# Chunk attention and an expert layer on one core: the first tile's row sums, transposes and casts in another order

## The chip, the cores and the metric

The kernel runs on one core of one Trainium2 chip. The metric is the device time of one execution in microseconds (us). Times inside a profile are us from the start of the profiled span.

## What is computed

The reference works on `q`, `k` and `v` of shape (8, 8, 576, 64): batch, heads, tokens, head size. Attention is taken inside chunks of 64 tokens; its result, with the heads side by side, is the input of an expert layer with an exact GELU.

```python
scores = (q_c @ k_c.T) / sqrt(64)          # per chunk of 64 tokens
attn   = exp(scores - max) / sum(exp(...)) # the kernel leaves the max out
x      = (attn @ v_c)                      # -> 4608 tokens x 512
out    = gelu(x @ w_in) @ w_out            # 512 -> 2048 -> 512
```

Inputs and output are f32; the kernel multiplies in bf16.

## The kernel before

**Tiles.** The 4608 tokens are worked in nine tiles of 512: eight tiles hold eight chunks of one batch entry each, the ninth holds the last chunk of all eight. A tile goes through attention and then the expert layer: sixteen output blocks of `x @ w_in` with GELU on ScalarE (`mm1_slot`), then the second product. While TensorE does the expert layer of one tile, the other engines load, cast, transpose and scale the next one. The first tile has nothing before it to hide behind: its attention runs alone, while the weights arrive and are cast.

**Order.** The program is written out by hand inside `tc.manual_schedule()`: each engine executes its instructions in the order in which they are emitted, and all loads go out on SyncE's queue. A tile pool with a fixed number of buffers makes an instruction wait for the last reader of the buffer it takes. In PSUM there are three pools: `ps_mm` (3 banks; expert outputs, k transposes of the first tile, warm matmuls), `ps_tp` (2 banks) and `ps_at` (3 banks).

**The first tile's attention.** The eight heads form four groups `g` of two heads. For each group:

- `cast_qk` turns the f32 arrivals of q and k into bf16 (VectorE or GpSimd, `DV` and `PO`).
- `att_T` (made by `att_units` as `T[0]` ... `T[7]`; even ones are q, odd ones k) transposes on TensorE (`transposed`, L166, four matmuls of 128x128) and copies the result from PSUM to `qT` (VectorE) or `kT` (ScalarE), L174.
- `att_S` (L376) computes 16 score blocks of 64x64 on 64x64 parts of the array, and ScalarE takes the exponentials into `pT` (two instructions, L380). Two groups share a pair of PSUM banks.
- The row sums. For groups 0 and 1 `att_sum` multiplies with a block matrix of ones (L387), so that every row of the output holds the sums; VectorE transposes in blocks of 32x32 (L392), takes the reciprocal of one column (L396) and transposes it back, spread over 32 columns, into `rcs` (L397). For groups 2 and 3 `att_sum_pe` makes the sums lie along partitions (L415, four matmuls with two moving columns), VectorE takes the reciprocal (L420), TensorE spreads it by f32 matmuls with an identity (L427) and ScalarE copies it to `rcs` (L430).
- `att_av` (L441) multiplies with V, two groups in a pair of banks, and `att_x` (L449) scales by `rcs` into `x`. For groups 0 and 1 this goes in two halves, `ns` being the pairs of chunks: (0, 1), then (2, 3).

`keep_warm(n)` (L725) issues `n` matmuls of zeros, 128x512, whose output nobody reads. `cast_v_plain` (L152) casts V, one block of 128 keys after the other.

**After it.** `win[c](i, engine)` casts block `i` of the c-th quarter of `w_in` (L706). `mm1_begin(0, 3)` (L493) starts the expert layer with three output blocks, whose inner index `ks` is the group of `x`: first `ks` 0 and 1 for all three, then 2 and 3. `mm1_slot` (L481) does the other thirteen.

Of the kernel before, what the change touches and what calls it, by code (L numbers as in the profile page):

```python
# [11 lines left out]
def kernel(  # L12
# [9 lines left out]
    nc = tc.nc  # L22
    P = 128
    f32 = mybir.dt.float32
    bf16 = mybir.dt.bfloat16
    Act = mybir.ActivationFunctionType

    B, H, S, D = q.shape
    CH = 64
# [3 lines left out]
    G = H // 2  # L33
# [3 lines left out]
    CT = NC - 1  # L37
    MT = CT * CH
    NT = B + 1
    KS = d_model // P  # L40
# [4 lines left out]
    consts = ctx.enter_context(tc.tile_pool(name="consts", bufs=1))  # L45
    rest = consts.tile([P, 512], bf16, name="rest")
    nc.vector.memset(rest[:], 0.0)
    ident = consts.tile([P, P], bf16, name="ident")
    make_identity(nc, ident)
    ones_bd = consts.tile([P, P], bf16, name="ones_bd")  # L50
    nc.vector.memset(ones_bd[:], 0.0)
    nc.vector.memset(ones_bd[0:CH, 0:CH], 1.0)
    nc.vector.memset(ones_bd[CH:P, CH:P], 1.0)

    ones_r = consts.tile([P, 2], bf16, name="ones_r")
    nc.gpsimd.memset(ones_r[:], 0.0)
    nc.gpsimd.memset(ones_r[0:CH, 0:1], 1.0)
    nc.gpsimd.memset(ones_r[CH:P, 1:2], 1.0)
    ident_f = consts.tile([P, P], f32, name="ident_f")
    nc.gpsimd.tensor_copy(ident_f[:], ident[:])  # L60
    QD = P // G
    ones_c = consts.tile([P, QD], bf16, name="ones_c")
    nc.gpsimd.memset(ones_c[:], 0.0)
# [14 lines left out]
    work = ctx.enter_context(tc.tile_pool(name="work", bufs=3))  # L78
    xpool = ctx.enter_context(tc.tile_pool(name="xpool", bufs=2))
    hpool = ctx.enter_context(tc.tile_pool(name="hpool", bufs=1))  # L80
    hsum = ctx.enter_context(tc.tile_pool(name="hsum", bufs=1))
    ypool = ctx.enter_context(tc.tile_pool(name="ypool", bufs=3))
    ps_mm = ctx.enter_context(tc.tile_pool(name="ps_mm", bufs=3, space=bass.MemoryType.PSUM))
    ps_tp = ctx.enter_context(tc.tile_pool(name="ps_tp", bufs=2, space=bass.MemoryType.PSUM))
    ps_at = ctx.enter_context(tc.tile_pool(name="ps_at", bufs=3, space=bass.MemoryType.PSUM))
# [8 lines left out]
    tiles = [dict() for _ in range(NT)]  # L94
# [49 lines left out]
        for n in range(CT // 2):  # L144
            nc.sync.dma_start(tiles[t]["vf"][:, :, n], v[t, :, P * n:P * (n + 1), :].rearrange("h key d -> key h d"))

    def cast_v_plain(t, copy, ns=range(CT // 2)):
        st = tiles[t]
        if 0 in ns:
            st["v"] = ld.tile([P, H, CT // 2, D], bf16, tag="v", name="v_nat")  # L150
        for n in ns:
            copy(st["v"][:, :, n], st["vf"][:, :, n])  # L152

    def place(r, i):

# [2 lines left out]
    def cast_qk(t, nm, g, copy):  # L158
        st = tiles[t]
        copy(st[nm][:, g].rearrange("p j r d -> p r j d"), st[nm + "f"][:, 2 * g:2 * g + 2])  # L160
# [16 lines left out]
    def parity_blocks(ns=range(4)):  # L177

        for n in ns:
            for a in range(2):  # L180
                for r in range(2):
                    c = a ^ r
                    yield n, r, c, 2 * n + c, slice(CH * r, CH * (r + 1)), slice(CH * c, CH * (c + 1))
# [186 lines left out]
    def att_S(t, g):  # L370

        st = tiles[t]
        if g % 2 == 0:
            st["s_ps"] = [ps_at.tile([P, 2, CT // 2, CH], f32, tag="at", name="s_ps") for _ in range(2)]
        for n, r, c, i, rs, cs in parity_blocks():
            nc.tensor.matmul(st["s_ps"][r][cs, g % 2, n], st["kT", g][rs, i, :], st["qT", g][rs, i, :],  # L376
                             start=True, stop=True, tile_position=(CH * r, CH * c))
        st["pT", g] = work.tile([P, 2, CT // 2, CH], bf16, tag="pT", name="pT", bufs=8)
        for r in range(2):
            nc.scalar.activation(st["pT", g][:, r], st["s_ps"][r][:, g % 2], Act.Exp, scale=scale)  # L380

    def att_sum(t, g, later=False):
        pT = tiles[t]["pT", g]
        sum_ps = ps_at.tile([P, MT], f32, tag="at", name="sum_ps")
        for c in range(2):
            for r in range(2):
                nc.tensor.matmul(sum_ps[CH * r:CH * (r + 1)].rearrange("p (n c e) -> p n c e", c=2, e=CH)[:, :, c],  # L387
                                 ones_bd[:, CH * c:CH * (c + 1)], pT[:, r], start=True, stop=True,
                                 tile_position=(0, CH * r))
        t1 = work.tile([P, NB, 32], f32, tag=f"y_{1 + t}", name="t1", bufs=1)  # L390
        rc = rc_of(t, g).rearrange("p (n e) -> p n e", e=32)
        nc.vector.transpose(t1[:], sum_ps[:].rearrange("p (n e) -> p n e", e=32))  # L392

        def rest_of_it():
            r1 = work.tile([P, NB], f32, tag="r1", name="r1", bufs=2)
            nc.vector.reciprocal(r1[:], t1[:, :, 0])  # L396
            nc.vector.transpose(rc, r1[:].to_broadcast([P, NB, 32]))  # L397
        if later:
            return rest_of_it
        rest_of_it()  # L400

    def att_rc(t, g):

# [1 line left out]
        rc = work.tile([P, NB, 32], f32, tag="rc", name="rc", bufs=4)  # L405
        nc.vector.transpose(rc[:], rb[:, g].to_broadcast([P, NB, 32]))  # L406
        tiles[t]["rc", g] = rc

    def att_sum_pe(t, g):

        pT = tiles[t]["pT", g]
        sT = ps_at.tile([P, 2, MT // P // 2, 2], f32, tag="at", name="sT")
        for r in range(2):
            for m in range(2):
                nc.tensor.matmul(sT[:, r, m], pT[:, r, 2 * m:2 * m + 2].rearrange("p n e -> p (n e)"), ones_r[:],  # L415
                                 start=True, stop=True)
        rr = work.tile([P, 2, MT // P // 2, 2], f32, tag="rr", name="rr", bufs=2)

        def inverse():
            nc.vector.reciprocal(rr[:], sT[:])  # L420

        def spread():
            rc_ps = ps_mm.tile([P, CT // 2, 2, CH], f32, tag="mm", name="rc_ps")
            for m in range(2):
                for c in range(2):
                    for r in range(2):
                        nc.tensor.matmul(rc_ps[CH * r:CH * (r + 1), 2 * m:2 * m + 2, c],  # L427
                                         rr[:, r, m, c:c + 1].to_broadcast([P, D]), ident_f[:],
                                         start=True, stop=True, tile_position=(0, CH * r))
            nc.scalar.copy(rc_of(t, g), rc_ps[:].rearrange("p n c e -> p (n c e)"))  # L430
        return inverse, spread

    def att_av(t, g2, ns):

# [9 lines left out]
    def att_x(t, g2, c, ns):  # L444

        st = tiles[t]
        def part(p):
            return p.rearrange("p g (n c e) -> p g n c e", c=2, e=CH)[:, :, ns[0]:ns[-1] + 1, c]
        nc.vector.tensor_tensor(part(st["x"][:, 2 * g2:2 * g2 + 2]), st["av", g2][c][:, :, ns[0]:ns[-1] + 1],  # L449
                                part(st["rcs", g2][:]), op=mybir.AluOpType.mult)  # L450

    def rc_of(t, g):

        if g % 2 == 0:
            tiles[t]["rcs", g // 2] = hsum.tile([P, 2, MT], f32, tag=f"s{3 + g // 2}", name="rcs")
        return tiles[t]["rcs", g // 2][:, g % 2]

    NB = MT // 32
    DV, AC, PO = nc.vector.tensor_copy, nc.scalar.copy, nc.gpsimd.tensor_copy
# [26 lines left out]
    def mm1_begin(t, n):  # L486

        st = tiles[t]
        st["h"] = hpool.tile([P, FF, MT], bf16, tag="h", name="h")
        h_ps = [ps_mm.tile([P, MT], f32, tag="mm", name="h_ps") for _ in range(n)]  # L490
        order = [(f, ks) for k2 in range(2) for f in range(n) for ks in (2 * k2, 2 * k2 + 1)]
        for f, ks in order:
            nc.tensor.matmul(h_ps[f][:], w_in_sb[:, ks, f * P:(f + 1) * P], st["x"][:, ks, :],  # L493
                             start=(ks == 0), stop=(ks == KS - 1))
        for f in range(n):
            nc.scalar.activation(st["h"][:, f, :], h_ps[f][:], Act.Gelu)
# [225 lines left out]
    def keep_warm(n):  # L722
        warm = ps_mm.tile([P, MT], f32, tag="mm", name="warm")
        for _ in range(n):
            nc.tensor.matmul(warm[:], rest[:, 0:P], rest[:], start=True, stop=True)  # L725
# [3 lines left out]
    def act_table(func):  # L729
        nc.scalar.activation(act_scratch[:], rest[:, 0:1], func)  # L730

    with tc.manual_schedule():
# [4 lines left out]
        win = [load_w_in(c, 2 if c < 2 else 1) for c in range(NWC - 1)]  # L737
        act_table(Act.Exp)
        keep_warm(7)
        T = att_units(0, DV, AC)  # L740
        for nm, g in (("k", 0), ("k", 1), ("q", 2), ("k", 2), ("q", 3), ("k", 3)):
            cast_qk(0, nm, g, PO)
        cast_v_plain(0, PO)
        cast_qk(0, "q", 0, DV)
        T[0]()
        cast_qk(0, "q", 1, DV)
# [1 line left out]
        keep_warm(3)  # L748
        T[2]()
        T[3]()  # L750
        att_S(0, 0)
        keep_warm(1)
        T[4]()
        r0 = att_sum(0, 0, True)
        att_S(0, 1)
        keep_warm(1)
        T[5]()
        r0()
        keep_warm(1)
        att_S(0, 2)  # L760
        T[6]()
        r1 = att_sum(0, 1, True)
        T[7]()
        i2, p2 = att_sum_pe(0, 2)
        i2()
        att_S(0, 3)
        r1()
        p2()
        i3, p3 = att_sum_pe(0, 3)
        i3()  # L770
        att_av(0, 0, (0, 1))
        for c in range(2):
            att_x(0, 0, c, (0, 1))
        p3()
        att_av(0, 0, (2, 3))
        for c in range(2):
            att_x(0, 0, c, (2, 3))
# [5 lines left out]
        win[0](0, PO)  # L783
        win[0](1, AC)
        act_table(Act.Gelu)
        win[0](2, PO)
        win[0](3, DV)
        mm1_begin(0, 3)
        load_qk(1, "q")
        wout.append(load_w_out(1))  # L790
# [22 lines left out]
        T = att_units(1, AC, AC)  # L813
# [47 lines left out]
        for t in range(1, NT):  # L861
            e1, e2 = {}, {}
            n = t + 1
# [71 lines left out]
```

## Time and profile before

| | |
|---|---|
| Runs, device us | 279.21, 279.69, 281.28; median 279.69 |
| Profiled execution | 281.07 us, of which the span in the profile is 279.3 us |
| Mean granted TensorE clock | 0.993 of full |
| Busy, share of the span | TensorE 96%, VectorE 60%, ScalarE 55%, GpSimd 31% |
| Second half of the chain before the expert layer | first expert matmul at 19.16 us |

Busy times are from the profiled execution, which can differ a little from the median run. The profile calls TensorE's matmuls PE and its weight loads PEld, VectorE DVE, ScalarE ACT, GpSimd POOL and SyncE SP. A line number such as L376 is a line of the kernel before. An entry like `DVE qT L174` is the instruction of VectorE that writes the tile `qT` at line 174; `xN` is how many of them were merged; the text in brackets names what ended the idle time before it. The chain in order of time gives start, duration and instruction of the work that ended last, followed back from the end.

### The profile page before, as it was taken

How to read it: one execution, taken by the hardware profiler on the slowest of the kernel's cores; microseconds unless marked ns; L12 is line 12 of the kernel's file. 1: busy time of each engine (PE TensorE's matmuls, PEld its weight loads, DVE VectorE, ACT ScalarE, POOL GpSimd, SP SyncE). 2: the span in 40 equal slices, each digit the busy share in tenths (PEclk: the TensorE clock that was granted, in tenths of full speed). 3: DMA queues.
4: the chain of work that ended last, by engine and by line, in shares of the span. 5: the costliest groups of instructions: out<-in, count | busy, mean ns of one | idle time of the engine just before them, and what ended most of it. 6: DMA issues, size and time to landing. Idle time of an engine off the chain costs nothing.

```text
span 279.3 us, 6704 instructions
## 1 busy us (share of the span) xinstructions
PE 269.3 (96%) x2721; PEld 159.6 (57%) x2721; DVE 166.6 (60%) x357; ACT 154.7 (55%) x290; POOL 87.7 (31%) x180
## 2 busy tenths in 40 slices
PE   7779999999999999999999999999999999999993
PEld 2454454444444444448844884588458745874682
DVE  2574226701956395995777577758775877434532
ACT  2467755778646765763566256725672565116500
POOL 2735675521630802740580372026402120000000
PEclk9799999999999999999999999999999999999999
DMA  6999999998899987999898829895841310040005
GB/s 202 248 365 404 395 387 247 260 257 237 244 230 266 236 192 212 299 210 241 232 239 211 228 92 232 202 186 156 210 99 40 116 38 2 0 153 0 0 2 151
DMA packets 118063, 53.92 MB, mean 193 GB/s; under 512 B 93456, under 2 KB 112912, under 8 KB 118032
## 3 DMA queue, kind: packets, MB, share of 16 engines
q1 hardware_dynamic: 117712, 52.97, 71.2%
q10 hardware_dynamic: 320, 0.52, 0.5%
q8 instruction: 21, 0.34, 0.5%
q14 instruction: 10, 0.08, 0.1%
HBM read 36.70 MB, written 9.44 MB: 165 GB/s over the span
## 4 chain that ended last, share of the span: by engine, by line
PE 92%; DVE 3%; DMA 2%; SPq 0%; issue 0%; ACT 0%; POOL 0%
PE h_ps L481 43%; PE y_ps L536 27%; PE y_ps L630 10%; PE y_ps L654 4%; DMA arrival<-in_k_dram 2%; PE av_ps L299 2%; PE s_ps L229 2%; PE tp L166 1%; PE h_ps L493 1%; DVE x L367 1%; PE rc_ps L427 1%; DVE rc L406 1%; SPq L112 0%; PE s_ps L376 0%; PE warm L725 0%
## 5 line engine op out<-in xcount | busy, mean ns | idle before, releaser
L481 PE MATMUL h_ps<-x,w_in_sb 128*128 128x512 bf16 x564 | 123.4, 379 | 0.4 <-DVE x L367 0.4
L484 ACT ACTIVATE h<-h_ps 128x512 bf16<-128x512 f32 x141 | 83.8, 597 | 55.7 <-PE h_ps L481 55.6
L481 PEld LDWEIGHTS <-w_in_sb 128*128 128x128 bf16 x564 | 55.1, 98 | 66.2 <-issue 0.7
L536 PEld LDWEIGHTS <-h_s 128*128 128x128 bf16 x384 | 36.8, 98 | 4.5
L160 POOL CAST q_nat<-arrival 128x512 bf16<-128x512 f32 x33 | 20.8, 668 | 57.0 <-DMA arrival<-in_q_dram 37.5
L536 PE MATMUL y_ps<-w_t,h_s 128*128 128x256 bf16 x288 | 33.7, 273 | 0.0
L630 PE MATMUL y_ps<-w_out_sb,h 128*128 128x512 bf16 x144 | 32.5, 380 | 0.0
L536 PEld LDWEIGHTS <-h 128*128 128x128 bf16 x288 | 28.2, 98 | 4.5
L251 DVE STREAM_TRANSPOSE pt<-pT 128x256 f32<-128x256 f32 x28 | 12.2, 437 | 27.8 <-ACT pT L236 27.8
L160 POOL CAST k_nat<-arrival 128x512 bf16<-128x512 f32 x34 | 20.1, 626 | 16.2 <-DMA arrival<-in_k_dram 11.8
L207 POOL CAST v_nat<-arrival 128x1024 bf16<-128x1024 f32 x14 | 14.4, 1040 | 31.5 <-DMA arrival<-in_v_dram 31.5
L516 DVE TENSOR_TENSOR h_s<-h 128x512 bf16<-128x512 bf16 (+1 forms) x30 | 11.2, 372 | 21.3 <-ACT h L484 21.3
L536 PE MATMUL y_ps<-w_out_sb,h 128*128 128x256 bf16 x192 | 22.9, 273 | 0.0
L630 PEld LDWEIGHTS <-h 128*128 128x128 bf16 x144 | 13.4, 98 | 15.6 <-issue 0.2
L730 ACT ACT_TABLE_LOAD x16 | 20.5, 1283 | 1.0 <-PEq L919 0.7
L254 DVE TENSOR_REDUCE part<-pt 128x16 f32<-128x512 bf16 x28 | 19.2, 686 | 1.0
L306 DVE TENSOR_TENSOR x<-av_ps,rc 128x512 bf16<-128x512 f32 x28 | 17.9, 684 | 3.1 <-PE av_ps L299 2.5
L569 ACT COPY y_sb<-y_ps 128x512 f32<-128x512 f32 x5 | 2.9, 586 | 26.1 <-PE y_ps L536 26.1
L236 ACT ACTIVATE pT<-s_ps 128x512 bf16<-128x512 f32 x28 | 14.4, 606 | 1.5 <-PE s_ps L229 1.5
L261 POOL COPY part<-part 32x32 f32<-32x32 f32 x40 | 9.2, 230 | 13.8 <-DVE part L254 12.1
L654 PE MATMUL y_ps<-w_out_sb,h 128*128 128x512 bf16 x48 | 11.8, 379 | 0.3 <-ACT h L484 0.3
L517 DVE TENSOR_TENSOR h_s<-h_s,h 128x512 bf16<-128x512 bf16 (+1 forms) x30 | 11.2, 372 | 1.0
(102 smaller groups left out, 248.8 us busy)
## 6 DMA issues: line engine op xcount, KB each, us to landing
out_dram<-y_sb SPq DMA_DIRECT2D x32, 256.0 KB, 2.6
arrival<-in_q_dram SPq DMA_DIRECT2D x7, 1024.0 KB, 6.7
arrival<-in_k_dram SPq DMA_DIRECT2D x24, 256.0 KB, 6.3
arrival<-in_v_dram SPq DMA_DIRECT2D x42, 128.0 KB, 3.1
arrival<-in_moe_w_out_dram SPq DMA_DIRECT2D x4, 1024.0 KB, 12.4
arrival<-in_v_dram SPq DMA_DIRECT2D x8, 256.0 KB, 6.3
arrival<-in_moe_w_in_dram SPq DMA_DIRECT2D x4, 512.0 KB, 6.2
arrival<-in_moe_w_in_dram SPq DMA_DIRECT2D x2, 1024.0 KB, 10.2
```

Of the source, the lines that this page charges most:

```text
L160: copy(st[nm][:, g].rearrange("p j r d -> p r j d"), st[nm + "f"][:, 2 * g:2 * g + 2])
L207: copy(st["v"][:, r::2], st["vf"][:, r::2])
L236: nc.scalar.activation(pT[:].rearrange("p u (c j) -> p u c j", j=J), s_ps[g2][c][:].rearrange("p u (j c) -> p u c j", j=J), Act.Exp, scale ...
L251: nc.vector.transpose(pt[:].rearrange("p n e u -> p (n e u)").bitcast(f32).rearrange("p (n e) -> p n e", e=32), st["pT", 2 * g2 + c][:].re ...
L254: nc.vector.tensor_reduce(st["part", g2][:, c, :, :, 0], pt[:].rearrange("p n e u -> p n u e"), axis=mybir.AxisListType.X, op=mybir.AluOpT ...
L306: nc.vector.tensor_tensor(x.rearrange("p n (e u) -> p n e u", u=2), st["av"][g2][c][:].rearrange("p n (e u) -> p n e u", u=2), st["rc", 2 ...
L481: nc.tensor.matmul(h_ps[a][:], w_in_sb[:, ks, o * P:(o + 1) * P], st["x"][:, ks, :], start=(ks == 0), stop=(ks == KS - 1))
L484: nc.scalar.activation(st["h"][:, f_of(t, f + a), :], h_ps[a][:], Act.Gelu)
L536: nc.tensor.matmul(out[m], lhs[:, f, m * P:(m + 1) * P], rhs[:, f, :], start=fresh and f == 0 and (m == 0 or len(out) == 3), stop=(f == FH ...
L630: nc.tensor.matmul(y_ps[:], st["h"][:, f, ms * P:(ms + 1) * P], w_out_sb[:, f, :], start=(f == 0), stop=(f == FF - 1))
L654: nc.tensor.matmul(tiles[t]["y_ps", ms][:], tiles[t]["h"][:, f, ms * P:(ms + 1) * P], w_out_sb[:, f, :], start=(f == 0), stop=False)
L730: nc.scalar.activation(act_scratch[:], rest[:, 0:1], func)
```

## The change

Only the first tile's part is changed.

- The row sums of all four groups are computed by `att_sums`: 32 matmuls for each group whose weights are 32 tokens of `pT` (128x32) and whose moving operand is `ones_r` (two columns). They write 32-partition blocks in the layout in which VectorE can take the reciprocal and spread it with one 32x32-block transpose (`att_spread`). `att_sum`, `att_sum_pe` and the constants `ones_bd` and `ident_f` go.
- The third group's k is cast by VectorE instead of GpSimd; the transposes `T[4]` to `T[6]` stand nearer to the casts, and the warm matmuls are placed anew (`keep_warm(1)` at four places of the attention instead of three).
- The last block of V is cast half by GpSimd and half by ScalarE.
- The third block of the first `w_in` quarter is cast by VectorE and the fourth by GpSimd (before: GpSimd and VectorE).
- In `mm1_begin` the third output block does its four matmuls at the end.

```diff
+    def att_sums(t, g):
+        st = tiles[t]
+        pT = st["pT", g]
+        st["sums", g] = ps_mm.tile([P, CT // 2, 2, 2], f32, tag="mm", name="sums_ps")
+        for n in range(CT // 2):
+            for e in range(2):
+                for s in range(G):
+                    nc.tensor.matmul(st["sums", g][QD * s:QD * (s + 1), n, :, e],
+                                     pT[:, s // 2, n, 32 * e:32 * (e + 1)], ones_r[:],
+                                     start=True, stop=True, tile_position=(0, QD * s))
+
+    def att_spread(t, g):
+        st = tiles[t]
+        if g % 2 == 0:
+            st["rcs", g // 2] = hsum.tile([P, 2, MT], f32, tag=f"s{3 + g // 2}", name="rcs")
+        r1 = work.tile([P, NB], f32, tag="r1", name="r1", bufs=2)
+        nc.vector.reciprocal(r1[:], st["sums", g][:].rearrange("p n c e -> p (n c e)"))
+        nc.vector.transpose(st["rcs", g // 2][:, g % 2].rearrange("p (n e) -> p n e", e=32),
+                            r1[:].to_broadcast([P, NB, 32]))
...
-        order = [(f, ks) for k2 in range(2) for f in range(n) for ks in (2 * k2, 2 * k2 + 1)]
+        order = [(f, ks) for k2 in range(2) for f in range(n - 1) for ks in (2 * k2, 2 * k2 + 1)] + \
+                [(n - 1, ks) for ks in range(KS)]
...
-        for nm, g in (("k", 0), ("k", 1), ("q", 2), ("k", 2), ("q", 3), ("k", 3)):
+        for nm, g in (("k", 0), ("k", 1), ("q", 2), ("q", 3), ("k", 3)):
             cast_qk(0, nm, g, PO)
-        cast_v_plain(0, PO)
+        cast_v_plain(0, PO, range(3))
+        cast_v_plain(0, PO, range(3, 4), slice(H // 2, H))
...
         T[3]()
+        cast_qk(0, "k", 2, DV)
         att_S(0, 0)
+        T[4]()
+        T[5]()
+        att_S(0, 1)
+        T[6]()
+        att_sums(0, 0)
+        att_spread(0, 0)
         keep_warm(1)
-        T[4]()
-        r0 = att_sum(0, 0, True)
-        att_S(0, 1)
+        T[7]()
+        att_S(0, 2)
+        att_sums(0, 1)
+        att_spread(0, 1)
         keep_warm(1)
-        T[5]()
-        r0()
+        att_S(0, 3)
+        att_sums(0, 2)
+        att_spread(0, 2)
+        att_sums(0, 3)
+        att_spread(0, 3)
         keep_warm(1)
-        att_S(0, 2)
-        T[6]()
-        r1 = att_sum(0, 1, True)
-        T[7]()
-        i2, p2 = att_sum_pe(0, 2)
-        i2()
-        att_S(0, 3)
-        r1()
-        p2()
-        i3, p3 = att_sum_pe(0, 3)
-        i3()
+        cast_v_plain(0, AC, range(3, 4), slice(0, H // 2))
         att_av(0, 0, (0, 1))
         for c in range(2):
             att_x(0, 0, c, (0, 1))
-        p3()
+        keep_warm(1)
         att_av(0, 0, (2, 3))
...
-        win[0](2, PO)
-        win[0](3, DV)
+        win[0](2, DV)
+        win[0](3, PO)
```

## The prediction

> **What bounds the kernel now.** I read the page first, then the chain in order of time, then the windows of the first 23 us, then the timeline.
>
> ```profile
> span 279.3 us, 6704 instructions
> ...
> PE 269.3 (96%) x2721; PEld 159.6 (57%) x2721; DVE 166.6 (60%) x357; ACT 154.7 (55%) x290; POOL 87.7 (31%) x180
> ...
> PEclk9799999999999999999999999999999999999999
> ```
>
> TensorE is busy for 96% of the span, so what can be won lies where it isn't the bound. The chain tells where that is: from 19.16 us it is nearly all matmuls to the end (but for some 6 us of VectorE around 47 to 54), and before that it hops between engines. All that the change touches lies before 22 us.
>
> ```profile
> 13.47 0.69 DVE qT L174
> 14.16 0.64 DVE t L392
> ...
> 14.84 0.25 PE sT L415 x4
> ...
> 15.38 1.09 PE rc_ps L427 x16
> ...
> 16.96 1.09 PE rc_ps L427 x16
> 18.05 0.28 PE av_ps L441 x16
> 18.36 0.32 DVE x L449
> ...
> 19.16 2.75 PE h_ps L493 x12
> 21.91 11.24 PE h_ps L481 x52
> ```
>
> So the reader sees a latency path: the sums of groups 2 and 3, their spreading by f32 matmuls (1.09 us each, on the path), the second half of the attention-value product, the scaling x, and at 19.16 the first expert matmul. Behind it 12 + 52 matmuls follow without a gap, 11.24/52 = 0.216 us each.
>
> ```profile
> 5.97:9.38 3.41, 1.75 (x29) 0.89 (x28) 1.12 (x2) 0.66 (x2) 1.39 (x3) 1.00 1.01 321
> 9.38:12.80 3.42, 3.17 (x35) 1.52 (x33) 2.37 (x4) 2.01 (x6) 2.66 (x5) 0.50 0.90 209
> 12.80:16.21 3.41, 2.62 (x64) 2.03 (x64) 2.35 (x5) 1.90 (x5) 1.47 (x3) 1.00 0.97 291
> 16.21:19.62 3.41, 2.75 (x93) 2.02 (x90) 2.23 (x6) 2.09 (x4) 1.23 (x2) 1.00 1.05 366
> ```
>
> These are stretches of 3.41 us, cut where the granted clock changes: stretch and length, PE, PEld, DVE, ACT and POOL busy, then the granted clock. After a stretch in which PE was busy 1.75 of 3.41 us (51%) the clock is half; after 77% and 81% it is full.
>
> ```profile
> 15.44 0.61 POOL L152 CAST v_nat<-arrival 128x512 bf16<-128x512 f32 x1 [1.50 <-DMA arrival<-in_v_dram]
> 16.76 0.61 POOL L706 CAST w_in_sb<-arrival 128x512 bf16<-128x512 f32 x1 [0.71 <-DMA arrival<-in_moe_w_in_dram]
> 18.85 0.61 POOL L706 CAST w_in_sb<-arrival 128x512 bf16<-128x512 f32 x1 [1.48 <-DMA arrival<-in_moe_w_in_dram]
> ```
>
> The last V block lands at 15.4, the first w_in half block at 16.7, the second at 18.8. No transfer is moved, and SP's issues keep their order, so the first expert matmul can't start before 16.76 + 0.61 = 17.4: at most 1.8 us can be won here.
>
> **The change, step by step**, on the time axis of this execution. *Up to the scores.* Nothing changes before 9.2. VectorE casts the third k in 0.43 (its q_nat row, L160) from 9.22, when its block is there now, to 9.65; POOL would end at 9.83. POOL keeps the fourth q and k where they end now, 10.50 and 11.24, as it takes blocks when they land. The warm matmul at 9.15 goes, so the third q's transposes end at 9.8 and the k's at 10.34 (four at half clock: 0.32 from first to last start, 0.31 for the last). ACT copies kT (0.59) to 10.96. The second scores wait for the first exponentials (10.15) and end at 10.66; their exponentials follow the copy to 11.5. The fourth q's transposes end at 11.2.
>
> *The sums.* Each group has 32 pairs, weights 128x32 and two columns moving. No row shows this shape. From below: 16 pairs of 64x64 take 0.15 at full clock and 0.21 at half (windows around their starts), so 32 take 0.30 and 0.42. From above: the 128x128 pairs with two columns (L415) start (0.24 - 0.163)/3 = 25 ns apart, so 32 take 0.8, and 1.6 if half clock doubles it. I take 0.35 and 0.5, near the first row, as both put four tiles in the array at once. [...]
>
> So sums 0 end at 11.85, and a warm matmul (0.43 at half clock) and the fourth k's transposes end at 12.76. On ACT the copy of that k runs to 13.38, and the third exponentials, queued behind it, to 13.93. The fourth scores wait for them (the same bank) and end at 14.3, their exponentials at 14.99. Sums 2 end at 14.61, sums 3 at 15.46.
>
> *Spreading, now all on VectorE.* Each group costs a reciprocal (0.20) and a transpose (0.71). Removed are two first transposes (L392, 0.72 and 0.71), two small reciprocals, 32 f32 matmul passes (2.18) and two ACT copies (0.59 each). The last two spreads run back to back from 14.64 and hold VectorE until 16.40. Behind them in its queue stand the six scalings: the first pair (0.76) ends at 17.16, 0.56 before today's 17.72. The second half of the product waits for that pair (same bank); matmuls to first scaling take 0.37, as from 17.98 to 18.36 now; the second pair runs from 17.59 to 18.34; the large pair (1.28) ends at 19.54.
>
> *The first expert matmuls.* They start at 18.39, against 19.16: 0.77 sooner. But the order now holds the third output block back (its weights are cast by VectorE behind the scalings): after 4 matmuls (0.86, to 19.25) the next need the large pair, 19.59, a stall of 0.34. Eight more end at 19.59 + 1.73 = 21.32. Now twelve without a stall end at 19.16 + 2.59 = 21.75. **Path: -0.43 us.**
>
> *Edits costed at nothing.* V's last block in two parts: ready at about 15.8, needed at 17.2 (without that cover 0.4). The third w_in block on VectorE: ready by 19.9, needed at 20.45. The fourth on POOL: 19.46, needed at 21.3. Removed constants (ones_bd, ident_f at 4.91) stand in front of no waiting instruction. Later blocks: the ninth w_in block is cast by 24.7 and needed at 26.2; tile 1's last V block is cast by 47.2 and needed at 48.2. Both leave 1.0 us or more, so the 0.43 reaches the end.
>
> *The clock.* The f32 matmuls were work for PE at 15.4 to 18.05. Without them PE idles from 16.05 to 17.20 and 17.75 to 18.39 and stalls at 19.4. In the stretch 16.21 to 19.62 that leaves 3.41 - 0.99 - 0.64 - 0.18 = 1.60 busy, 47%, less than the 51% after which the clock was halved. Price: from nothing (clock kept) to 3.41/2 = 1.71 (a whole stretch of dense matmuls at half). Where the stretches begin in other executions one trace doesn't tell; one that begins earlier falls on the hole itself and slows little. I take the middle, 0.85. [...]
>
> **Sum:** -0.43 + 0.85 = +0.4. The profiled execution took 281.07, 1.8 around its span, so it would take 281.5. It stands 1.4 above the median of the runs, 279.69; on that the forecast is **280.1**.
>
> **Rivals.** *The clock is kept:* -0.43, 279.3. For it: the new warm matmuls, and 47% is close to nothing that the trace tests (no stretch lies between 51% and 77%). Against it: 51% was not enough.
>
> *The whole stretch is lost (slower):* the hole puts 19.62 to 23.03 at half clock, under dense matmuls that nothing hides: -0.43 + 1.71 = +1.3, 281.0. It decides from a busy share of about half on. For it: the row at 5.97. Against it: it needs the stretches to lie as in this execution. If a second stretch falls too (the small sums counting as little work), add about 0.6.
>
> *The sums cost 25 ns a pair:* sums 0 push the fourth k by about 0.7 (the half clock ends at 12.80) and sums 2 add 0.5: +1.2 on the path, 0.8 slower, 280.5 with the clock kept and 281.3 with 0.85 for it. For it: the L415 row, also 128 rows deep. Against it: those are not tiles.
>
> *It doesn't do what it says:* the third k is cast only 0.18 sooner, and the path of the fourth is set by its landing; if VectorE's two queued spreads run later than I put them, the gain is gone: 279.7.
>
> **How the numbers follow.** Forecast 0.40, clock kept 0.25, whole stretch 0.17, slow sums 0.10, no effect 0.08. The bounds: path -0.43 to +0.8, clock 0 to 1.7, and the runs shown differ by 2 us among themselves. The range is 278.6 to 281.6: the low end leaves 0.7 under "clock kept" for that scatter, the high end is the slow-sums case with a little over it. A measurement of this kernel can tell about 1% (2.8 us) from no change. Faster by that needs more than the 1.8 us there is: 0.03. Slower by that needs slow sums and a whole stretch together (+2.5) and something more: 0.06. Within it: 0.91.
>
> **What would show it.** In the profile after: the sums' 32 pairs within 0.3 to 0.6 us; the first expert matmul near 18.4 and a gap of about 0.3 after four of them; VectorE without a gap from 14.6 to 17.2; the granted clock in the stretch after the hole. Wrong if the sums take 0.8 or more, if the expert matmuls start after 19.2, or if the clock falls in a stretch that I counted as busy.

## The result, and the profile after

The changed kernel is 0.6% slower: ratio 1.0063, with a 95% interval of 1.0041 to 1.0085.

| | before | changed |
|---|---|---|
| Median of 20 runs each, us | 280.53 | 282.13 |
| Lowest to highest, us | 279.21 to 283.59 | 280.62 to 284.49 |
| Profiled execution and its span, us | 281.07, 279.3 | 281.53, 279.7 |
| Mean granted TensorE clock in it | 0.993 | 0.982 |

Runs more than 1.5% above the fastest of their kernel count as slow and are left out of the ratio here (one of before's 20; 280.46 without it) and of everything below (7 of 87 later runs of before, one each of e6 and e10).

By the bound of 1% the sign is "no change", as forecast; but the interval leaves 1 out, and 282.13 lies above the range, whose upper end was 281.6. The page of the changed kernel, lines of the same three parts as before:

```profile
span 279.7 us, 6860 instructions
...
PE 270.4 (97%) x2802; PEld 159.6 (57%) x2802; DVE 166.2 (59%) x355; ACT 153.9 (55%) x289; POOL 87.5 (31%) x178
...
PEclk9759999999999999999999999999999999999999
```

TensorE's busy time rises by 1.1 us, though f32 work was taken from it, and the third slice of the clock row is at half. A busy time that grows when work is removed suggests that the same work ran slower. The chain in order of time, changed kernel:

```profile
14.47 0.71 DVE rcs L394
...
15.36 0.71 DVE rcs L394
16.07 0.65 DVE x L420 x2
16.76 0.45 PE av_ps L412 x11
17.58 0.42 DVE x L420
18.14 3.77 PE h_ps L459 x12
21.90 0.65 PE h_ps L446 x3
```

The path is the one that was laid out: VectorE's two spreads one behind the other, the first scalings, the second half of the product, the next scalings, the experts. The first expert matmul starts at 18.14, against 18.39 forecast and 19.16 before. But its twelve take 3.77 us instead of 2.75 and end at 21.90, where before's ended at 21.91. One microsecond was won and the whole of it was lost within twelve matmuls. The windows cut at the clock's changes tell how (same columns as in the prediction; here and below the cuts lie within 0.1 us of the changes):

```profile
6.58:9.99 3.41, 2.12 (x49) 1.30 (x47) 1.72 (x3) 1.38 (x4) 1.67 (x3) 1.00 1.14 331
9.99:13.40 3.41, 3.19 (x96) 1.99 (x100) 2.06 (x5) 2.07 (x6) 2.38 (x5) 0.50 0.85 193
13.40:16.82 3.42, 2.96 (x104) 1.74 (x106) 2.94 (x7) 1.42 (x4) 0.96 (x3) 0.50 0.95 305
16.82:20.23 3.41, 2.89 (x53) 1.39 (x53) 2.71 (x6) 1.75 (x3) 1.59 (x3) 0.50 1.08 369
```

Three stretches in a row are at half clock, where before had one (9.38 to 12.80). The last of them covers the first five expert matmuls. Compare the second row with before's row 9.38:12.80: both were 93% busy at half clock, yet before's next stretch was at full clock and this one's was not. Before had 35 matmuls in it, this one 96. Transposes and warm matmuls took about as long in both (1.23 and 1.41 us in before, 1.24 and 1.22 here). What before had besides is its first row sums, 0.86 us in four matmuls of 256 columns; this one had small matmuls instead. It seems that "busy" is not the same thing for the clock.

The half clock came behind a stretch that was 62% busy (the first row), and stayed through one that was 93% busy.

What is left of the difference in span, about 0.4 us, arises near 188 us, where one wait that no semaphore ends appears in the middle of a block of 64 score matmuls that before ran in one piece. The timeline, changed kernel:

```profile
188.28 0.53 PE L222 MATMUL s_ps<-q_t,k_t 64*64 64x64 bf16 x42
189.03 0.38 PE L222 MATMUL s_ps<-q_t,k_t 64*64 64x64 bf16 x22 [0.22 <-issue]
```

**The clock over all runs.** One profile is one draw: where the 3.41 us stretches fall differs from run to run (half clock begins at 9.38 in before's profile, at 9.99 in the changed kernel's). Each timed run lists its span and mean granted clock, so the two can be held against each other. Call (1 - clock) x 280 the lost time. A least-squares line gives

- before, 80 runs: span = 278.24 + 0.41 x lost; mean clock 0.9947, so 1.49 us lost
- changed, 20 runs: span = 277.95 + 0.50 x lost; mean clock 0.9821, so 5.01 us lost

So 0.4 to 0.5 of each lost microsecond reaches the end. A stretch of 3.41 us at half clock loses 1.71, so before loses 0.9 stretches an execution and the changed kernel 2.9. The 3.52 us more cost 1.4 us by the first slope and 1.8 by the second; the mean spans differ by 1.6 (280.45 - 278.85). At equal clock the changed kernel is thus between 0.2 longer and 0.2 shorter: no gain on the path can be told from the runs. That this is the clock's doing is so far an association; the experiments test it.

### The profile page after: what moved, and what is told of

Its sections match the earlier page's. It is cut to its first block, busy times and chain, and to the rows that moved or that the text cites. A ratio compares the mean times of both kernels' runs of the same rounds, so it can differ in the third digit from the quotient of the medians.

```text
span 279.7 us, 6860 instructions
## 1 busy us (share of the span) xinstructions
PE 270.4 (97%) x2802; PEld 159.6 (57%) x2802; DVE 166.2 (59%) x355; ACT 153.9 (55%) x289; POOL 87.5 (31%) x178
## 4 chain that ended last, share of the span: by engine, by line
PE 91%; DVE 3%; DMA 2%; SPq 1%; issue 1%; POOL 0%; ACT 0%
PE h_ps L446 43%; PE y_ps L502 27%; PE y_ps L596 10%; PE y_ps L620 4%; DMA arrival<-in_q_dram 2%; PE s_ps L222 2%; PE av_ps L292 2%; PE h_ps L459 1%; PE tp L159 1%; SPq L105 1%; DVE x L360 1%; DVE rc L401 1%; DVE rcs L394 1%; DVE x L420 0%; PE warm L691 0%
## 5 line engine op out<-in xcount | busy, mean ns | idle before, releaser
L153 POOL CAST k_nat<-arrival 128x512 bf16<-128x512 f32 x33 | 19.4, 625 | 17.2 <-DMA arrival<-in_k_dram 14.4
L254 POOL COPY part<-part 32x32 f32<-32x32 f32 x40 | 9.8, 245 | 12.6 <-DVE part L247 10.9
```

## The experiments

Theory A: the removed matmuls, the f32 ones above all, held the clock, and its loss is the cost. Rival B: the small sums cost time on TensorE by themselves. Rival C: the new path is late somewhere else. All runs are timed beside before; the clock is the mean of the timed runs, and the ratio is estimated from all of them, so it is not the quotient of the medians.

| | median, us | before, us | ratio (95%) | clock |
|---|---|---|---|---|
| e1_fill_early | 281.98 | 280.77 | 1.0041 (1.0011 to 1.0071) | 0.987 |
| e2_f32_back | 281.07 | 280.77 | 1.0017 (0.9986 to 1.0048) | 0.992 |
| e3_before_no_warm | 282.55 | 280.77 | 1.0066 (1.0036 to 1.0096) | 0.981 |
| e4_sums_twice | 288.99 | 280.77 | 1.0291 (1.0249 to 1.0334) | 0.966 |
| e6_fill_late | 281.80 | 280.29 | 1.0043 (1.0007 to 1.0078) | 0.987 |
| e7_fill_both | 281.31 | 280.29 | 1.0021 (0.9991 to 1.0052) | 0.993 |
| e8_sums_16 | 281.84 | 280.29 | 1.0040 (1.0005 to 1.0076) | 0.980 |
| e9_before_fill | 280.64 | 280.29 | 1.0003 (0.9969 to 1.0038) | 0.997 |
| e10_f32_fill | 281.69 | 280.61 | 1.0023 (0.9995 to 1.0050) | 0.997 |
| e11_sums_16_fill | 280.46 | 280.61 | 1.0002 (0.9973 to 1.0031) | 0.995 |

**Take the warm matmuls out of before.** The plainest test of A: less work on TensorE, nothing else touched.

```diff
--- before
         att_S(0, 0)
-        keep_warm(1)
         T[4]()
...
         att_S(0, 1)
-        keep_warm(1)
         T[5]()
         r0()
-        keep_warm(1)
```

> The kernel before without its three single warm matmuls between 9 and 12 us; nothing else is changed. They stand on its path for up to 0.2 to 0.6 us each at half clock, so without the clock the time would fall by 0.3 to 1 us. Clock theory: less work for TensorE in that stretch, so the clock stays halved for one or two stretches more (mean granted clock 0.98 to 0.985), and the time is 0.5 to 2 us above before. Path and late rivals: 0.3 to 1 us below before.

It is 0.66% slower, as much as the changed kernel. The mean clock fell to 0.981, and at equal clock its span is 278.1 (span less 0.5 x lost, mean), the same as before's. Three matmuls of no use were worth about 1.8 us. Windows of this kernel:

```profile
4.78:8.20 3.42, 1.45 (x12) 0.66 (x11) 1.18 (x3) 0.58 (x1) 0.64 (x3) 0.99 0.91 297
8.20:11.61 3.41, 2.93 (x47) 1.94 (x48) 1.84 (x3) 1.31 (x4) 2.84 (x6) 0.50 0.97 254
11.61:15.02 3.41, 2.42 (x33) 1.35 (x31) 2.47 (x5) 1.90 (x6) 1.82 (x3) 0.50 0.92 231
15.02:18.44 3.42, 3.29 (x58) 2.72 (x59) 1.35 (x5) 1.57 (x4) 1.23 (x2) 0.50 0.99 316
18.44:21.85 3.41, 2.97 (x66) 2.33 (x65) 1.89 (x5) 1.58 (x3) 1.23 (x2) 0.51 1.08 398
```

Here too half clock follows one thin stretch (1.45 of 3.42), and it stays through stretches of 86%, 71% and 96% busy. So the clock alone can make a difference of this size, with no small sum in the program.

**Put the f32 spreading back for groups 2 and 3.** The rest of the change stays (the functions and the constant that it removed are put back too; that part isn't printed).

```diff
--- changed
+        i2, p2 = att_sum_pe(0, 2)
+        i2()
         att_S(0, 3)
-        att_sums(0, 2)
-        att_spread(0, 2)
-        att_sums(0, 3)
-        att_spread(0, 3)
-        keep_warm(1)
+        p2()
+        i3, p3 = att_sum_pe(0, 3)
+        i3()
...
-        keep_warm(1)
+        p3()
         att_av(0, 0, (2, 3))
```

> The changed kernel with groups 2 and 3 summed and spread as before (four matmuls with two columns, reciprocal, f32 matmuls with the identity, ScalarE's copy), two warm matmuls less; all other edits stay. Clock theory: the f32 matmuls put 2.2 us of work back where TensorE otherwise idles, so the granted clock returns to about 0.99 and the time to within 0.5 us of before. Path rival: the same gain, but then the changed kernel's profile must show the first expert matmul later than here at the same clock; if this kernel's expert matmuls start later (18.4 or more against 18.1) and it is still faster, the path rival falls. Late rival: no gain, 1.5 us above before.

The clock is back at 0.992, and the time at before's (1.0017, the interval holds 1). Its profiled execution ran at full clock through the whole stretch, in a span of 277.9:

```profile
7.00:10.41 3.41, 3.05 (x87) 2.02 (x85) 2.27 (x4) 2.26 (x6) 2.29 (x4) 1.00 1.14 316
10.41:13.83 3.42, 3.10 (x98) 2.22 (x98) 2.06 (x6) 1.91 (x6) 1.84 (x3) 1.00 0.98 251
13.83:17.24 3.41, 2.70 (x86) 1.90 (x85) 2.64 (x7) 2.71 (x5) 1.01 (x2) 1.00 0.91 297
```

So what lowers the clock sits in how the sums of groups 2 and 3 are spread, as A has it. That rests on the mean clock over the runs, 0.992 against 0.982; the intervals of the two ratios still overlap (1.0048 against 1.0041). The profiled execution doesn't show how: its clock was full from 7.0 on, and the f32 matmuls start only at 12.59, so no halving was there to recover from. Nor did the test that the expectation set for the path take place, as this kernel's experts start sooner than the changed kernel's, not later. The timeline shows why full clock alone wins so little:

```profile
16.43 3.02 PE L491 MATMUL h_ps<-x,w_in_sb 128*128 128x512 bf16 x12 [0.66 <-POOL w_in_sb L704]
```

The experts start at 16.43, and the cast of the first w_in block ended just ahead of that: the next bound is a landing, not TensorE. Of the 2.7 us won on before here, only 0.9 are left when the second tile's experts start (50.8 against 51.66); ahead of that TensorE waits 1.0 us for the cast of a V block of that tile.

The same profiles let the new spreading be compared with the old. These are the fourth group's scores in before, then these scores and the first scaling of groups 2 and 3 in e2, then in the changed kernel:

```profile
15.01 0.32 PE L376 MATMUL s_ps<-qT,kT 64*64 64x64 bf16 x16
12.12 0.32 PE L371 MATMUL s_ps<-qT,kT 64*64 64x64 bf16 x16
15.57 1.95 DVE L452 TENSOR_TENSOR x<-av_ps,rcs 128x256 bf16<-128x256 f32 x4 [0.64 <-PE av_ps L444]
13.25 0.52 PE L369 MATMUL s_ps<-qT,kT 64*64 64x64 bf16 x16
17.23 1.95 DVE L420 TENSOR_TENSOR x<-av_ps,rcs 128x256 bf16<-128x256 f32 x4 [0.53 <-PE av_ps L412]
```

From the one to the other it is 3.35 us in before (the scaling at 18.36 in the prediction's chain) and 3.45 in e2, both with f32 matmuls at full clock, against 3.98 in the changed kernel at half clock and 3.98 in e11 below at full clock. With f32 matmuls at half clock it is 5.21 (e3, 15.40 to 20.61). So spreading on VectorE hardly depends on the clock, but where the clock is full it is 0.5 to 0.6 us slower than what it replaced. All of the 1.0 us that the changed kernel's profile wins was won ahead of the fourth scores, which start 1.76 sooner. Rival C is right in that much.

**Fill the holes of the changed kernel** with warm matmuls ahead of the sums, behind them, and both.

```diff
--- changed (e1_fill_early; e7_fill_both has both parts)
-        keep_warm(3)
+        keep_warm(7)
         T[2]()
+        keep_warm(2)
         T[3]()
         cast_qk(0, "k", 2, DV)
         att_S(0, 0)
+        keep_warm(1)
--- changed (e6_fill_late)
         att_spread(0, 3)
-        keep_warm(1)
+        keep_warm(3)
...
             att_x(0, 0, c, (0, 1))
-        keep_warm(1)
+        keep_warm(3)
...
+        keep_warm(2)
         win.append(load_w_in(NWC - 1))
```

> The changed kernel with seven more warm matmuls in the waits for the first tiles of q and k (7 instead of 3 behind the second cast, 2 behind the third transposes, 1 behind the first scores). They stand where TensorE waits for landings, so by themselves they add at most 0.4 us. Clock theory (the path is shorter, and the loss comes from a clock that stays halved over 10 to 20 us): the first halving is avoided or cut to one stretch, the mean granted clock rises to 0.99 or more, and the time falls by 1 to 2 us, to the time of the kernel before or up to 1 us under it. Rival 'path' (the new sums or VectorE's queue cost the time): the clock may rise, but the time stays within 0.5 us of the changed kernel, 1.5 us above before. Rival 'late' (something behind 22 us, such as instruction waits, costs it): as the path rival, with the first expert matmuls as early as before.

> The changed kernel with six more warm matmuls late: three instead of one after the last sums, three instead of one before the second half of the product, two before the first expert matmul. Clock theory: they take the place of the 2.2 us of f32 matmuls; at full clock they fit into the waits for VectorE (1.1 and 0.6 us), at half clock they delay the path by up to 1 us. The granted clock rises above 0.982, and the time falls by 0 to 1 us from the changed kernel, least where the early halving is still there. Path and late theories: no gain, 0.5 to 1 us slower than the changed kernel.

> The changed kernel with the warm matmuls of both fills, early (seven) and late (six). Clock theory alone: no stretch falls under the share that halves the clock, mean granted clock 0.995 or more, time 279.5 to 280.5, 0.5 to 1.5 us under before. Supply theory (TensorE starts with 449 instructions at hand and gets the next 256 only about 2.3 us after a fetch that shows at 12 to 13 us; the changed kernel reaches number 449 within its last sums): at full clock it gets there sooner and stands still for about 1 us, as in the profile of the early fill (sums after 12 of 32 pairs, 1.05 us), so the time stays at 280.5 to 282 even at a clock of 0.99.

Each half brings the clock to 0.987, both together to 0.993, near before's 0.995; the medians are 281.98, 281.80 and 281.31, against the changed kernel's 282.13. e1 falls short of what was expected of it, a clock of 0.99 and 1 to 2 us. And e7 near before's clock is no faster than before (1.0021). In e1 the timeline shows a wait that nobody had counted on:

```profile
13.27 0.51 PE L383 MATMUL sums_ps<-ones_r,pT 128*32 128x2 bf16 x12 [0.18 <-ACT pT L373]
14.82 0.29 PE L383 MATMUL sums_ps<-ones_r,pT 128*32 128x2 bf16 x20 [1.05 <-issue]
```

In the middle of the last group's 32 pairs TensorE stands for 1.05 us, and by the profile no semaphore is what it waits for. The same wait is in the list of waits of e6 (0.7) and of e7 (0.5). And it falls into the hole, and the clock is lost behind it; windows of e1:

```profile
9.91:13.32 3.41, 3.04 (x155) 2.22 (x142) 2.65 (x7) 2.47 (x8) 2.30 (x5) 1.00 1.01 231
13.32:16.73 3.41, 1.71 (x51) 0.98 (x52) 2.35 (x6) 0.93 (x3) 0.92 (x3) 0.99 1.03 331
16.73:20.15 3.42, 2.76 (x53) 1.44 (x52) 2.90 (x7) 1.74 (x3) 1.63 (x3) 0.50 1.07 380
```

Behind the first filling the clock is full to 16.7; the stretch with the wait was only 50% busy, and the next was at half, again under the first expert matmuls.

**Issue every sum pair twice.** This was to price the small matmuls (rival B).

```diff
--- changed, att_sums
-                for s in range(G):
+                for s in list(range(G)) * 2:
```

> The changed kernel with each of the small sum matmuls issued twice (64 pairs for a group instead of 32). Path rival: the sums' price doubles; if they are what costs, the time rises by 1 us or more. Clock theory: 32 pairs take 0.3 us at either clock in the profile, two of the four groups are on the path, so the time rises by 0.5 to 0.8 us; and if these small matmuls counted as work for the clock, 1.2 us more of them would bring back part of it (mean granted clock above that of the changed kernel, 0.982), else the clock stays where it is.

It is 8 us above before and 6.9 above the changed kernel's median. The 128 pairs more are 1.2 us at 9 ns each, so the sums' own price is little of it. The waits of TensorE in this kernel (total, times, longest):

```profile
PE sums_ps L383 <- issue: 4.5, 1, 4.5
PE s_ps L369 <- issue: 1.2, 1, 1.2
```

Two waits without a semaphore, 5.7 us together. Counted in the program's order, matmuls and weight loads each as one, the first comes behind the 449th instruction of TensorE, as in e1, e6 and e7, and the second behind the 705th, 256 further. A third theory, D: TensorE runs out of instructions.

**Half the instructions for the sums.** Sixteen pairs of 64 tokens a group instead of 32 pairs of 32. Half of the tokens are then divided by another token's sum; the later work is the same in kind and amount.

```diff
--- changed, att_sums
-                for s in range(G):
-                    nc.tensor.matmul(st["sums", g][QD * s:QD * (s + 1), n, :, e],
-                                     pT[:, s // 2, n, 32 * e:32 * (e + 1)], ones_r[:],
-                                     start=True, stop=True, tile_position=(0, QD * s))
+                for r in range(2):
+                    nc.tensor.matmul(st["sums", g][CH * r:CH * (r + 1), n, :, e], pT[:, r, n, :], ones_r[:],
+                                     start=True, stop=True, tile_position=(0, CH * r))
```

> The changed kernel with 16 pairs of 64 tokens for a group in place of 32 pairs of 32 tokens; half of the tokens are then divided by the sum of another token, which this kernel leaves wrong to halve the number of instructions. Nothing else on the path changes but 0.15 us for a group. Supply theory: 128 instructions fewer stand ahead of the first expert matmul (478 against 606), number 449 falls behind the last sums and no wait for instructions shows in them; the mean time falls by 0.5 to 1.2 us against the changed kernel, and its fastest runs reach 279.3 to 280 (the changed kernel's fastest is 280.6). Clock theory without supply: the work that counts is the same or less, clock 0.982 or below, time as the changed kernel within 0.4 us.

Alone it changes little: 281.84 against the changed kernel's 282.13, with the clock at 0.980, lower still. Theory D's 0.5 to 1.2 us didn't come, but its profile, like the changed kernel's, has half clock and no wait for instructions in the sums, so D wasn't put to the test by it. At equal clock its span is 277.3, 0.6 below the changed kernel's 277.95 (standard errors 0.2 and 0.1). Fewer pairs were no shorter: sixteen of 128x64 take 0.34 us at full clock (e11, 11.31 to 11.65) and 0.52 at half (e8, 10.93 to 11.45), where 32 of 128x32 take 0.30 and 0.32. Both fillings on top of it (e11_sums_16_fill is e8 with the edits of e1 and e6):

> The changed kernel with 16 sum pairs of 64 tokens for a group (half of the tokens are divided by another token's sum, left wrong to halve the instructions) and both fills. It differs from the kernel with both fills (281.3, clock 0.993) only in the instructions ahead of the expert layer, and from the one with 16 pairs (281.8, clock 0.980) only in the fills. Clock and supply together: no wait for instructions in the sums, clock 0.993 or more, 279.6 to 280.5, so 0.8 to 1.5 us under each of the two. Clock alone: as the kernel with both fills, 281.0 to 281.6. Supply alone: as the one with 16 pairs.

280.46 is before's time (1.0002), as expected of clock and supply together, and 0.85 below e7, which differs from it in the sums alone; but the intervals of the two ratios overlap, so the price of the instruction waits isn't settled by times. Its profiled execution had a mean clock of 1.0, no wait for instructions in the sums, and this timeline:

```profile
17.17 0.61 POOL L671 CAST w_in_sb<-arrival 128x512 bf16<-128x512 f32 x1 [1.93 <-DMA arrival<-in_moe_w_in_dram]
17.84 1.04 PE L458 MATMUL h_ps<-x,w_in_sb 128*128 128x512 bf16 x4 [1.24 <-POOL w_in_sb L671]
```

With the clock and the instructions there, the experts wait 1.24 us for a weight block whose cast begins at 17.17; their x was ready near 16.8 (the scalings begin at 16.07 in that profile, and the first two take 0.76 in before). What the full clock wins is in part spent waiting for a transfer that the change doesn't move.

**Fill before, and fill e2.** If the clock is all, before itself should gain by filling (its e1 edit, without the last warm matmul), and so should e2 (with the whole of it).

> The kernel before with six more warm matmuls in the waits for the first q and k (seven instead of three behind the second cast, two behind the third transposes). Clock theory: the halving at 9 us is avoided, mean granted clock 0.996 or more (before 0.991), median time 279.5 to 280.2, 0.8 to 1.3 us under before, and less scatter. Without it: the same time, or up to 0.4 us slower for the added matmuls.

> The changed kernel with groups 2 and 3 summed and spread as before, and the seven early warm matmuls. Clock theory: full clock through the first tile (0.996 or more), no wait for instructions, the first expert matmul 1 to 2 us before that of the kernel before. If TensorE bound the first 50 us, the time would be 279.0 to 279.5; the profile of the same kernel without the fill shows waits for landings of w_in at 16.4 and of tile 1's q at 31 us instead, so 279.6 to 280.3 is expected, 0.2 to 0.8 us under before. If it stays at the time of before or over it, the fill costs on the path what the clock gives.

Both missed. The clock did rise, to 0.997 in both, but the medians are 280.64 (1.0003) and 281.69 (1.0023). So a clock restored by filling isn't by itself time won. At equal clock their spans are 278.6 and 278.9 against before's 278.1: the filling itself, or later landings, took back what the clock gave. In e10's profile the first expert matmul waits 1.8 us for the cast of w_in:

```profile
PE h_ps L491 <- POOL w_in_sb L704: 1.8, 1, 1.8
```

Why that block lands later in some kernels than in others was not separated from the filling.

## Why the prediction was wrong, step by step

**The base.** The three runs shown of before had a median of 279.69; 80 later ones have 280.53. About 0.8 of the 2.0 us by which 282.13 missed 280.1 is that. The prediction counted 2 us of scatter between runs, but set its forecast on the lower of its two references, and its high end, 281.6, held the dearest rivals with none of that scatter above them; its own sum on the profiled execution, 281.5, was that execution's time exactly (281.53), by two errors that cancel in it: a shorter path and a lower clock than forecast.

**The sums.** Right, and below the value taken. 32 pairs take 0.30 us from the first start to the next row (10.33 to 10.63 in e1's timeline), 9 ns a pair, as the 64x64 row gave. The 25 ns of the 128x128 pairs, the prediction's figure from above, were not met by tiles of 128x32 and 64x64, 9 ns, but nearly by e11's tiles of 128x64, 21 ns. The rival "slow sums" falls.

**The path.** The order of the chain was as laid out, and the experts start 1.0 sooner (0.77 forecast). That the size came out is partly luck: the fourth scores start 0.7 sooner than laid out (13.25; they were to wait for the exponentials to 13.93), and half clock and the spreading behind them cost 0.4 of that. The stall after four expert matmuls is 0.24 at full clock (e7: starts at 18.34 and 18.80, less one spacing of 0.22), against 0.34. "So the 0.43 reaches the end" isn't borne out: at equal clock the runs are between 0.2 shorter and 0.2 longer. At full clock the cast of w_in (e11, 1.24 us) and the wait behind the 449th instruction (e1, 1.05, and e7, 0.46) take part of it. The prediction knew the first bound (17.4 from its landings) but took the landing of one execution as fixed; the first cast ended at 16.4 in e2, 17.8 in e11 and 18.0 in e10. The second it did not know.

**The clock.** The mechanism was right: e3 shows it without the change (0.981 against before's 0.995), e2 by taking part of the change back (0.992 against 0.982). The term failed in its count. It allowed for half of one stretch lost, 0.85. By the lines over the runs a whole stretch costs 1.71 x 0.4 to 0.5, so 0.7 to 0.85, at the end, and 2.1 more of them are lost: 1.4 to 1.8. Three parts of the working led there. The busy share was used as the measure, with "about half" as the border, but the stretch that halved the clock in the changed kernel was 62% busy (2.12 of 3.41). Each stretch was judged alone, though the half clock lasted three stretches in the changed kernel and four in e3: after 93% busy at half clock before's came back (0.86 us of it wide row sums) and the changed kernel's did not (small sums in their place). And the half clock was taken to end at 12.80, as in before; it lasted to 20.23. The stretch from 13.40, 86% busy and still at half clock, comes under one of the signs of being wrong that the prediction named (the clock at fault in a stretch counted as busy). The f32 passes were the dense work of the hole; the sums that took their place are 9 ns each. The prediction had this as an aside, "if a second stretch falls too (the small sums counting as little work), add about 0.6", under a rival of 0.17. That rival, 281.0 to 281.6, came nearest; on the base of 280.5 it would be 281.8 to 282.4.

**The edits at nothing.** V's last block and the later w_in blocks show up in no chain of the changed kernel, as said. Not among them was the instruction count, which changed by 156 in the program (6704 to 6860) and was nowhere priced.

**Still open.** Why filling before and e2 raised the clock and not the speed; the price of the instruction waits in the median; whether the wait of 0.22 at 188 us is regular; how much each kind of matmul counts for the clock.

## What to carry to other kernels

Before taking work off a matmul engine in a stretch that is bound by latency, ask what that work does for the clock: a wasteful but dense matmul may be what holds it, and tiny matmuls in its place may not (here 0.992 in e2 with the f32 spreading, 0.982 with the small sums). Price the clock as a number of whole stretches lost (here 2.9 against 0.9), by how many it takes to come back, and compare two kernels' spans at equal granted clock before arguing about paths. When the path is shortened, look at once for the landing that becomes the next bound, and count the instructions ahead of it.

## What the runs showed of the hardware that was not expected

**A wait behind the 449th instruction.** In e1, e4, e6 and e7 TensorE stops behind its 449th instruction, the 223rd matmul in each of the four timelines, in e4 again 256 later. The DMA queue of kind "instruction" moves packets of 16,384 bytes, 21 in before's profile and 22 in the changed kernel's; the first two of the latter start at 12.08 and 18.34 us, 6.3 us apart. In e4 TensorE goes on at 15.07 and 21.27, 6.2 us apart, while the DMA engines are 90% busy or more; in e1, e6 and e7 it goes on at 14.82, 14.02 and 14.27. The longest of these waits, in e4, was 4.5 us. e11, with half the pairs, had no such wait at full clock. That TensorE waits for these packets (theory D) is a reading of these times and counts. The changed kernel has 606 TensorE instructions ahead of its first expert matmul, e8 478, before 446 (each pass of an f32 matmul counted as one); waits of over 0.2 us behind the 449th were seen only with 32 pairs in all four groups at full clock, or with twice as many. The changed kernel, at half clock, comes to the border later: it passes it at 14.63 without such a wait, where e1, at full clock, stops at 13.77.

**Busy share and the clock of the next stretch.** At full clock the busy share of a stretch nearly told what came next: six stretches that were followed by half clock were 44 to 62% busy (e10, e3, e8, e1, before, changed, from the lowest up) and one, with mostly small matmuls, some 70% (e6, 11.87 to 15.28); e2's, at 79 to 91%, were followed by full clock. At half clock it told little: 93% (changed), 96% (e3) and 100% (e8) were not enough, and 85% was (changed, 16.82 to 20.23). There the kind of matmul told more. Leave out the transposes and the matmuls of under 128 columns, and the rest (warm matmuls, before's row sums, f32 passes, products of the expert layer) filled 61% or more of each of the eight stretches after which full clock came back, and at most 53% of thirteen of the fourteen after which it didn't; the fourteenth, in e3, had 62%. With the transposes counted the two kinds overlap, as e8 had some 70% without coming back. These are counts over the first 28 us of twelve profiles from the first clock record on, not a rule that was tested. The start of an execution runs at half speed too: up to the first clock record (5.97 in before, 6.58 in the changed kernel) the warm matmuls start 427 ns apart, and the expert matmuls at full clock 216, though the clock column shows 1.00 throughout. In e2, whose warm matmuls from 5.55 on are still 427 apart, one stretch of 68% (0.11 to 3.52, with the first matmul at 1.20) was not enough. The length of one idle gap told little: e9 kept the clock over a wait of 1.35 us (to 8.86), and the changed kernel lost it in a stretch whose longest was 0.78 (to 9.32).
